# Top-k attention with a phase mixer: work three units ahead, marks in tiles of two batches, one step fewer in the weights' conversion, the sums' constant added by GpSimd

## The chip, the cores and the metric

The kernel runs on one NeuronCore of one Trainium2 chip. The time is the device time of one execution, in microseconds; lower is better. The kernel before takes 1268.95 us, the median of three runs (1268.45 to 1269.72).

## The reference

There are 8 batches, 8 heads, 576 positions and 64 channels per head; the mixer works on 512 channels. Everything is float32 at the reference's level; the four weight matrices reach the kernel as 64-bit floats and are converted on the chip.

```python
scores = scale * np.matmul(q, k.transpose(0, 1, 3, 2))
kth = np.partition(scores, -top_k, axis=-1)[..., -top_k:-top_k + 1]   # top_k = 32
scores = np.where(scores >= kth, scores, -1000000000.0)
scores = scores - np.max(scores, axis=-1, keepdims=True)
attn = np.exp(scores)
attn = attn / (np.sum(attn, axis=-1, keepdims=True) + 1e-09)
x = np.matmul(attn, v)            # then heads side by side: (batch, seq, 512)
theta = x @ w_theta
y = einsum('ts,bsd->btd', w_tok_r, x * np.cos(theta)) + einsum('ts,bsd->btd', w_tok_i, x * np.sin(theta))
u = x + y
return u + np.maximum(u @ w_ch, 0.0)
```

## The kernel before

**Units.** Two heads make a pair, so a batch has 4 pairs. A pair's 576 queries are cut into four blocks of 128 for both heads and one block in which the 64 remaining queries of both heads lie together: five units, of which the last has half the work. There are 160 units. The loop in `pipeline` walks over them; in step `i` different units are at different stages, in the order of the letters in `ORDER`.

**One unit's way.** `scores` multiplies queries and keys on TensorE (PE) in two passes (`kh`, `kl`) into a PSUM tile `ps_score`, of which there are two places, and ScalarE (ACT) copies it to a tile `e` in SBUF (tag `e`, `EBUFS` places, shared with the loaded pairs). `fold` compares quarters of a row on VectorE (DVE) (L295 to L298): the largest of each four go to the list `lst`, the others to `lo1`, which has two places. `pick` takes the best eights of `lo1` into the list (L303). `threshold` ranks the list in four rounds of MAX8 and MATCH_REPLACE8 (L317, L323) and ends with L327; GpSimd (POOL) makes the limits from it (L328). `penalize` has ACT and POOL push the scores below the limit down (L336, L338). `exponent` is on ACT and leaves the sums (L348). `turn` transposes on PE (`pt`, L363) and ACT copies to `at`; `mix_values` multiplies with the values (`px`).

The scores and the fold of unit `i + AHEAD` are issued in step `i`, the pick of unit `i + 1`, the ranking of unit `i`. `FOLDS` is the number of places for `lst`.

**Marks.** A short list could miss a value. POOL copies the smallest entries of each picked eight and the ranks of each unit to `marks`, one slot per head and query block (L304, L330). After the last unit, DVE compares all 288 slots at once and reduces the answer to one flag; a branch redoes everything in a plain way if the flag is set.

**Mixer.** When a batch's attention is done, `mixer` normalizes with the reciprocals of the sums (`rinv`, L446 and L447), computes angles (`pth`, L518), sine and cosine, the token products (`py`, L633; DVE adds them with `settle`, L609) and the output products (`po`, L660; DVE empties them with `give`, L614). It is a generator: `turn` advances it by some matmuls after each transposed head, so a batch's mixer runs beside the next batch's attention. The last batch's mixer has nothing beside it and runs in three passes of halved operands (`halve`, L409 on ACT, L410 on POOL or DVE).

**Weights.** `widen_steps` converts one of 17 weight blocks in each step from the third on. `size` is in PSUM; DVE raises it to `SMALLEST` (L156) and shifts it into the bits of a float32 (L157); POOL puts the parts together (L159, L160).

The order within each engine is not the order of the code: a planner with modelled durations lays out one fixed row of instructions per engine; each engine then works through its row in order.

Of the kernel before, what the change touches and what calls it, by code (L numbers as in the profile page):

```python
# [18 lines left out]
P = 128  # L19
EBUFS = 10  # L20
NQP = 1
WSTART = 2
AHEAD = 2
# [3 lines left out]
FOLDS = 3  # L27
BESTS = 4
M_TOK = 400
# [8 lines left out]
SMALLEST = 1.125 * 2.0  # L38
# [6 lines left out]
def topk_attention_phase_mixer(  # L45
# [30 lines left out]
    NSLOT = B * NPAIR * (2 * NJ + 1)  # L76
# [17 lines left out]
    marks = const.tile([P, NSLOT, NE + 4], F32, name="marks")  # L94
    nc.gpsimd.memset(marks[:, :, :NE], -1.0)
    nc.gpsimd.memset(marks[:, :, NE:], 0.0)
# [21 lines left out]
    def widen_steps():  # L118
# [26 lines left out]
        def convert(i):  # L145
# [7 lines left out]
            for c in range(0, n, m):  # L153
                size = ps_m.tile([P, 512], F32, tag="m", name="size")[:, :m]
                nc.scalar.activation(size, sign[:, c : c + m], AF.Abs, scale=2.0**16)
                nc.vector.tensor_scalar(size, size, SMALLEST, None, op0=ALU.max)  # L156
# [143 lines left out]
    def pick(u):  # L300
        for i, (lo, hi) in enumerate(EXTRA):
            for w in range(u.n):
                nc.vector.max(u.lst[:, w, QS + i * 8 : QS + i * 8 + 8], u.lo1[:, w, lo:hi])  # L303
        nc.gpsimd.tensor_copy(marks[:, u.slot : u.slot + u.n, :NE], u.lst[:, : u.n, QS + 7 :: 8])  # L304
# [4 lines left out]
    def threshold(u):  # L309
# [19 lines left out]
        if not u.full:  # L329
            nc.gpsimd.tensor_copy(marks[:, u.slot : u.slot + n, NE:], top[:, :n, 7 : LB - 1 : 8])  # L330
        yield

# [107 lines left out]
    def mixer(bt, split=False, beside=False):  # L440
# [4 lines left out]
        for rows, js in ((P, slice(0, NJ)), (REM, slice(NJ, NJ + 1))):  # L445
            nc.vector.tensor_scalar(rinv[:rows, js], sums[:rows, js], 1e-9, None, op0=ALU.add)  # L446
            nc.vector.reciprocal(rinv[:rows, js], rinv[:rows, js])  # L447
# [228 lines left out]
    def pipeline():  # L676
# [5 lines left out]
        def unit(i):  # L682
            if not 0 <= i < total:
                return None
            if i not in units:
# [4 lines left out]
                units[i] = Unit(b, batches[b], p, j, pairs[g], g * (2 * NJ + 1) + 2 * j, False)  # L690
# [30 lines left out]
        for i in range(total + 3):  # L721
# [30 lines left out]
            for c in ORDER:  # L752
                steps[c]()
            if i == 0:
# [8 lines left out]
        worst = const.tile([P, 1], F32, name="worst")  # L763
        flag_f = const.tile([1, 1], F32, name="flag_f")
        kept = const.tile([P, 1], F32, name="kept")
        over = wk2.tile([P, NSLOT, NE + 3], BF16, tag="lo1", name="over")
        nc.vector.tensor_tensor(
            over,
            marks[:, :, : NE + 3],
            marks[:, :, NE + 3 :].to_broadcast([P, NSLOT, NE + 3]),  # L770
            op=ALU.is_ge,
        )
        nc.vector.tensor_reduce(kept, over[:, :, NE:], axis=AX.XY, op=ALU.min)
        nc.vector.tensor_reduce(worst, over[:, :, :NE], axis=AX.XY, op=ALU.max)
        nc.vector.tensor_tensor(worst, worst, kept, op=ALU.is_ge)
        pf = ps_m.tile([P, 512], F32, tag="m", name="pf")
# [74 lines left out]
```

## Time and profile before

| | |
|---|---|
| median of three runs | 1268.95 us (1268.45 to 1269.72) |
| profiled execution | 1273.75 us |
| its span, first to last instruction | 1271.9 us |
| busy: PE, DVE, ACT, POOL | 1137.0, 1139.2, 1021.9, 686.0 us |
| mean granted clock of PE | 0.953 of full speed |
| 0 to 260 us | attention of batch 0 and the weights, then the first mixer starts |
| 260 to 1118 us | attention of one batch beside the mixer of the one before |
| from 1177 us | transposes of the last units, then the last mixer alone |

Shares over the whole span mix these stages. What matters in each is which engine has no idle time, and what the others wait for. "Busy" of PE contains the modelled ends of overlapping matmuls. Lines such as L446 are lines of the kernel before.

### The profile page before, as it was taken

How to read it: one execution, taken by the hardware profiler on the slowest of the kernel's cores; microseconds unless marked ns; L12 is line 12 of the kernel's file. 1: busy time of each engine (PE TensorE's matmuls, PEld its weight loads, DVE VectorE, ACT ScalarE, POOL GpSimd, SP SyncE). 2: the span in 40 equal slices, each digit the busy share in tenths (PEclk: the TensorE clock that was granted, in tenths of full speed). 3: DMA queues.
4: the chain of work that ended last, by engine and by line, in shares of the span. 5: the costliest groups of instructions: out<-in, count | busy, mean ns of one | idle time of the engine just before them, and what ended most of it. 6: DMA issues, size and time to landing. Idle time of an engine off the chain costs nothing.

```text
span 1271.9 us, 23007 instructions
## 1 busy us (share of the span) xinstructions
PE 1137.0 (89%) x6293; PEld 849.5 (67%) x6293; DVE 1139.2 (90%) x5049; ACT 1021.9 (80%) x2098; POOL 686.0 (54%) x944
## 2 busy tenths in 40 slices
PE   3666679799999998999989998999999998998998
PEld 3554455578667875687657775677757775676688
DVE  7999999989999899989999799989999899988263
ACT  4999888987799868997789868997879868996361
POOL 2677774763565535664456444664546535756130
PEclk7677789899999999999999999999999999999899
DMA  7255432332323133332322233323313333200001
GB/s 198 73 159 159 118 92 63 93 85 76 113 70 81 53 106 94 93 84 76 113 56 75 66 113 94 93 67 94 112 32 84 82 103 103 74 10 1 38 2 40
DMA packets 71020, 106.14 MB, mean 83 GB/s; under 512 B 13920, under 2 KB 32608, under 8 KB 70880
## 3 DMA queue, kind: packets, MB, share of 16 engines
q1 hardware_dynamic: 70880, 104.57, 30.1%
q8 instruction: 52, 0.85, 0.3%
q14 instruction: 88, 0.72, 0.2%
HBM read 38.40 MB, written 9.44 MB: 38 GB/s over the span
## 4 chain that ended last, share of the span: by engine, by line
PE 44%; DVE 29%; ACT 15%; DMA 4%; POOL 3%; issue 3%; SPq 1%; ACTq 0%; POOLq 0%; DVEq 0%
PE py L633 17%; PE px L393 7%; PE ps_score L259 6%; DVE lst L323 6%; DVE best L317 6%; DVE lst L303 5%; PE pt L363 5%; PE pth L518 5%; ACT e L348 3%; DVE lo L296 3%; PE po L660 2%; ACT e L268 2%; ACT pen L336 2%; POOL e L338 2%; DVE ps_score L295 2%
## 5 line engine op out<-in xcount | busy, mean ns | idle before, releaser
L338 POOL TENSOR_TENSOR e<-e,pen 128x576 f32<-128x576 f32 x288 | 365.5, 1285 | 153.9 <-ACT pen L336 152.9
L317 DVE MAX8 best<-lst 128x8 f32<-128x122 f32 (+3 forms) x1152 | 286.1, 287 | 0.7
L633 PE MATMUL py<-w,z 128*128 128x288 f32 x1008 | 267.4, 408 | 0.2
L348 ACT ACTIVATE e<-e,lim 128x576 f32<-128x576 f32 x288 | 224.7, 782 | 28.9 <-POOL e L338 27.9
L259 PE MATMUL ps_score<-kh,q 128*128 128x288 f32 x512 | 185.2, 377 | 58.5 <-ACT e L268 36.8
L336 ACT ACTIVATE pen<-e,lim 128x576 bf16<-128x576 f32 x288 | 210.2, 776 | 32.3 <-POOL lim L328 31.6
L323 DVE MATCH_REPLACE8 lst<-best,lst 128x122 f32<-128x122 f32 (+2 forms) x864 | 230.9, 273 | 0.0
L363 PE MATMUL pt<-ident,e 128*128 128x128 f32 x1152 | 185.4, 288 | 35.1 <-ACT e L348 31.4
L633 PEld LDWEIGHTS py<-w,z 128*128 128x128 f32 x1008 | 182.5, 191 | 40.9 <-POOL z L550 0.7
L303 DVE MAX8 lst<-lo 128x8 f32<-128x72 f32 (+1 forms) x864 | 209.3, 291 | 0.1
L363 PEld LDWEIGHTS pt<-ident,e 128*128 128x128 f32 x1152 | 143.0, 147 | 76.8 <-ACT e L348 39.4
L268 ACT COPY e<-ps_score 128x576 f32<-128x576 f32 x256 | 161.3, 640 | 30.0 <-PE ps_score L259 22.0
L365 ACT COPY at<-pt 128x512 f32<-128x512 f32 x256 | 148.5, 587 | 35.4 <-PE pt L363 34.5
L393 PE MATMUL px<-at,vt 128*64 128x320 f32 (+1 forms) x1024 | 161.0, 433 | 10.0 <-ACT at L368 7.0
L259 PEld LDWEIGHTS ps_score<-kh,q 128*128 128x128 f32 x512 | 102.1, 199 | 87.2 <-ACT e L268 46.7
L259 PE MATMUL ps_score<-kl,q 128*128 128x288 f32 x512 | 151.7, 311 | 0.0
L660 PE MATMUL po<-xt,w 128*128 128x288 f32 x448 | 127.3, 415 | 6.6 <-DVE ot L614 6.6
L393 PEld LDWEIGHTS px<-at,vt 128*64 128x64 f32 x1024 | 78.8, 144 | 74.2 <-issue 14.3
L296 DVE TENSOR_TENSOR lo<-ps_score,e 128x576 f32<-128x576 f32 (+1 forms) x160 | 109.6, 685 | 0.0
L259 PEld LDWEIGHTS ps_score<-kl,q 128*128 128x128 f32 x512 | 103.4, 202 | 5.9 <-issue 1.4
L295 DVE TENSOR_TENSOR ps_score<-ps_score,e 128x288 f32<-128x288 f32 (+1 forms) x160 | 67.9, 424 | 43.5 <-ACT e L268 38.0
L518 PE MATMUL pth<-w,xt 128*128 128x512 f32 x224 | 103.9, 598 | 0.0
(131 smaller groups left out, 1926.6 us busy)
## 6 DMA issues: line engine op xcount, KB each, us to landing
kh<-hi SPq DMA_DIRECT2D x124, 144.0 KB, 2.6
kl<-raw SPq DMA_DIRECT2D x124, 144.0 KB, 2.6
raw<-in_qT_dram SPq DMA_DIRECT2D x31, 288.0 KB, 3.0
raw<-in_kT_dram SPq DMA_DIRECT2D x31, 288.0 KB, 3.2
q<-hi SPq DMA_DIRECT2D x62, 144.0 KB, 2.6
q<-raw SPq DMA_DIRECT2D x62, 144.0 KB, 2.7
vt<-in_v_dram SPq DMA_DIRECT2D x32, 256.0 KB, 3.2
out_dram<-ot SPq DMA_DIRECT2D x28, 288.0 KB, 2.1
```

Of the source, the lines that this page charges most:

```text
L259: nc.tensor.matmul(out[:, at : at + n], l, r, start=(i == 0), stop=(i == len(mm) - 1), skip_group_check=True)
L268: nc.scalar.copy(u.x[:, :, keys], u.ps[:, :, :HS])
L303: nc.vector.max(u.lst[:, w, QS + i * 8 : QS + i * 8 + 8], u.lo1[:, w, lo:hi])
L317: nc.vector.max(top[:, w, best], part[w])
L323: nc.vector.match_replace(out=rest, in_to_replace=top[:, w, best], in_values=part[w], imm_value=LOWEST)
L336: nc.scalar.activation(pen[:, w], u.x[:, w], AF.Relu, bias=u.lim[:, w, 0:1], scale=-STEEP)
L338: nc.gpsimd.tensor_sub(u.x[:, w], u.x[:, w], pen[:, w])
L348: nc.scalar.activation(u.x[:, w], u.x[:, w], AF.Exp, bias=u.lim[:, w, 1:2], scale=SCALE, accum_out=acc)
L363: fixed(nc.tensor.transpose(pt[:, c], e[:, w, at0 : at0 + P], ident))
L393: nc.tensor.matmul(px[sl, :n], pr["vt"][:, kb, sl], pr["at"][:, a, kb], start=(kb == 0), stop=False, skip_group_check=True)
L518: fill(nc.tensor.matmul(th[j][: l.shape[-1]], l, r, **pos))
L633: fill(nc.tensor.matmul(py[:, :HS], l, r, start=(i == 0), stop=(i == len(mm) - 1)))
```

## The change

There are five parts. `AHEAD` goes from 2 to 3, with one more place for `e` tiles and one more for lists. `marks` is no longer one constant tile of 288 slots, but a tile of 72 slots for two batches, of which two are alive; `judge` compares and reduces one such tile two steps after its last unit, so four times, and a short reduction joins the four answers at the end. The two memsets of `marks` go. In the weights' conversion ACT scales by another power of two, with which DVE's raising (L156) is left out. In the mixer, the constant 1e-9 is added to the sums by POOL in place, with a broadcast tile `least`, and DVE only takes the reciprocal.

```diff
-EBUFS = 10
+EBUFS = 11
...
-AHEAD = 2
+AHEAD = 3
...
-FOLDS = 3
+FOLDS = 4
 BESTS = 4
+MARKED = 2
...
-SMALLEST = 1.125 * 2.0
...
-    NSLOT = B * NPAIR * (2 * NJ + 1)
+    NSLOT = MARKED * NPAIR * (2 * NJ + 1)
...
-    marks = const.tile([P, NSLOT, NE + 4], F32, name="marks")
-    nc.gpsimd.memset(marks[:, :, :NE], -1.0)
-    nc.gpsimd.memset(marks[:, :, NE:], 0.0)
+    worst = const.tile([P, B // MARKED], F32, name="worst")
+    kept = const.tile([P, B // MARKED], F32, name="kept")
+    least = const.tile([P, 1, 1], F32, name="least")
+    nc.vector.memset(least, 1e-9)
...
-                nc.scalar.activation(size, sign[:, c : c + m], AF.Abs, scale=2.0**16)
-                nc.vector.tensor_scalar(size, size, SMALLEST, None, op0=ALU.max)
+                nc.scalar.activation(size, sign[:, c : c + m], AF.Abs, scale=2.0**-112)
                 nc.vector.tensor_scalar(bits[:, c : c + m], size.bitcast(I32), 3, None, op0=ALU.logical_shift_left)
...
-        nc.gpsimd.tensor_copy(marks[:, u.slot : u.slot + u.n, :NE], u.lst[:, : u.n, QS + 7 :: 8])
+        if u.slot == 0:
+            u.batch["marks"] = wk2.tile([P, NSLOT, NE + 4], F32, tag="marks", name="marks")
+        nc.gpsimd.tensor_copy(u.batch["marks"][:, u.slot : u.slot + u.n, :NE], u.lst[:, : u.n, QS + 7 :: 8])
...
+    def judge(marks, i):
+        over = wk2.tile([P, NSLOT, NE + 3], BF16, tag="lo1", name="over")
+        nc.vector.tensor_tensor(
+            over,
+            marks[:, :, : NE + 3],
+            marks[:, :, NE + 3 :].to_broadcast([P, NSLOT, NE + 3]),
+            op=ALU.is_ge,
+        )
+        nc.vector.tensor_reduce(kept[:, i : i + 1], over[:, :, NE:], axis=AX.XY, op=ALU.min)
+        nc.vector.tensor_reduce(worst[:, i : i + 1], over[:, :, :NE], axis=AX.XY, op=ALU.max)
...
         for rows, js in ((P, slice(0, NJ)), (REM, slice(NJ, NJ + 1))):
-            nc.vector.tensor_scalar(rinv[:rows, js], sums[:rows, js], 1e-9, None, op0=ALU.add)
-            nc.vector.reciprocal(rinv[:rows, js], rinv[:rows, js])
+            tiny = least[:rows].to_broadcast([rows, js.stop - js.start, H])
+            nc.gpsimd.tensor_add(sums[:rows, js], sums[:rows, js], tiny)
+            nc.vector.reciprocal(rinv[:rows, js], sums[:rows, js])
...
+            done = unit(i - 2)
+            if done and done.j == NJ and done.p == NPAIR - 1 and done.bq % MARKED == MARKED - 1:
+                judge(done.batch["marks"], done.bq // MARKED)
...
-        over = wk2.tile([P, NSLOT, NE + 3], BF16, tag="lo1", name="over")
...
-        nc.vector.tensor_reduce(kept, over[:, :, NE:], axis=AX.XY, op=ALU.min)
-        nc.vector.tensor_reduce(worst, over[:, :, :NE], axis=AX.XY, op=ALU.max)
         nc.vector.tensor_tensor(worst, worst, kept, op=ALU.is_ge)
+        nc.vector.tensor_reduce(worst[:, :1], worst, axis=AX.X, op=ALU.max)
```

Lines of the changed kernel are shifted: its L319, L325, L329 are L317, L323, L327 of before, L351 is L338, L423 is L410, L455 is L442, L461 is L447, L494 is L480, L623 is L609, L628 is L614; its L460 is the new addition.

**Conversion.** DVE's row where the second weight block is converted, first of the kernel before. `lst` and `best` belong to units that are being ranked, numbers tell the units apart.

```order
L323 MATCH_REPLACE lst_439<-best_440,lst_439 128x102
L156 TENSOR_SCALAR size_463<-size_463 128x512
L323 MATCH_REPLACE lst_439<-best_440,lst_439 128x102
L295 TENSOR_TENSOR lo1_531<-ps_score_523,e_516 128x2x144
L296 TENSOR_TENSOR lo1_531<-ps_score_523,e_516 128x2x288
L327 TENSOR_REDUCE best_291<-best_291 128x2
L317 MAX best_364<-lst_363 128x8
L317 MAX best_440<-lst_439 128x8
L157 TENSOR_SCALAR room_228<-size_463 128x512
```

The same place of the changed kernel:

```order
L325 MATCH_REPLACE lst_315<-best_316,lst_315 128x158
L297 TENSOR_TENSOR lst_461<-ps_score_455,lo1_463 128x2x144
L298 TENSOR_TENSOR lo1_463<-ps_score_455,lo1_463 128x2x144
L157 TENSOR_SCALAR room_251<-size_485 128x512
L303 MAX lst_461<-lo1_463 128x8 x2
L325 MATCH_REPLACE lst_386<-best_387,lst_386 128x102 x2
L329 TENSOR_REDUCE best_223<-best_223 128x2
```

The instruction L156 between ACT's `size` and the shift L157 is gone; the shift stands between the fold and the pick of a unit.

**Middle.** DVE's row in the third batch, kernel before, from the last rounds of one unit (list 6709) to the first of the next (list 6800):

```order
L323 MATCH_REPLACE lst_6709<-best_6710,lst_6709 128x158 x2
L317 MAX best_6710<-lst_6709 128x8 x2
L609 TENSOR_TENSOR xt_4022<-py_6425,xt_4022 128x288
L327 TENSOR_REDUCE best_6710<-best_6710 128x2
L295 TENSOR_TENSOR ps_score_6794<-ps_score_6794,e_6787 128x2x144
L295 TENSOR_TENSOR lo1_6802<-ps_score_6794,e_6787 128x2x144
L296 TENSOR_TENSOR lo1_6802<-ps_score_6794,e_6787 128x2x288
L297 TENSOR_TENSOR lst_6800<-ps_score_6794,lo1_6802 128x2x144
L298 TENSOR_TENSOR lo1_6802<-ps_score_6794,lo1_6802 128x2x144
L303 MAX lst_6800<-lo1_6802 128x8 x2
L317 MAX best_6801<-lst_6800 128x8 x2
L303 MAX lst_6800<-lo1_6802 128x8 x4
```

The changed kernel, from the pick of one unit (list 6546) on:

```order
L303 MAX lst_6546<-lo1_6548 128x8 x2
L319 MAX best_6547<-lst_6546 128x8 x2
L303 MAX lst_6546<-lo1_6548 128x8 x4
L325 MATCH_REPLACE lst_6546<-best_6547,lst_6546 128x102 x2
L295 TENSOR_TENSOR ps_score_6617<-ps_score_6617,e_6610 128x2x144
L319 MAX best_6547<-lst_6546 128x8 x2
L295 TENSOR_TENSOR lo1_6625<-ps_score_6617,e_6610 128x2x144
L296 TENSOR_TENSOR lo1_6625<-ps_score_6617,e_6610 128x2x288
L325 MATCH_REPLACE lst_6546<-best_6547,lst_6546 128x122 x2
L297 TENSOR_TENSOR lst_6623<-ps_score_6617,lo1_6625 128x2x144
L298 TENSOR_TENSOR lo1_6625<-ps_score_6617,lo1_6625 128x2x144
L303 MAX lst_6623<-lo1_6625 128x8 x2
```

Before, a unit's fold, pick and four rounds stand in one piece and the next unit's fold follows. Now the next unit's fold (list 6623) stands between the second and the third round. In PE's row 234 score matmuls stand ahead of the first angle matmul of the first mixer in both kernels, and 276 before and 284 now ahead of its first token matmul.

**End of attention, DVE.** DVE's row from the last reduction of the last unit's ranking on, kernel before:

```order
L327 TENSOR_REDUCE best<-best 128x1
L609 TENSOR_TENSOR xt<-py,xt 128x288
L767 TENSOR_TENSOR over<-marks 128x1728
L446 TENSOR_SCALAR rinv<-sums 128x32
L773 TENSOR_REDUCE kept<-over 128x1
L774 TENSOR_REDUCE worst<-over 128x1
L447 RECIPROCAL rinv<-rinv 128x32
L775 TENSOR_TENSOR worst<-worst,kept 128x1
L609 TENSOR_TENSOR xt<-py,xt 128x288
L446 TENSOR_SCALAR rinv<-sums 64x8
L447 RECIPROCAL rinv<-rinv 64x8
L614 SCALAR_TENSOR_TENSOR ot<-po,xt 128x288 x8
```

The changed kernel, from the same reduction on:

```order
L329 TENSOR_REDUCE best<-best 128x1
L623 TENSOR_TENSOR xt<-py,xt 128x288
L337 TENSOR_TENSOR over<-marks 128x432
L343 TENSOR_REDUCE kept<-over 128x1
L344 TENSOR_REDUCE worst<-over 128x1
L783 TENSOR_TENSOR worst<-worst,kept 128x4
L784 TENSOR_REDUCE worst<-worst 128x1
L623 TENSOR_TENSOR xt<-py,xt 128x288
L461 RECIPROCAL rinv<-sums 128x32
L623 TENSOR_TENSOR xt<-py,xt 128x288
L461 RECIPROCAL rinv<-sums 64x8
L628 SCALAR_TENSOR_TENSOR ot<-po,xt 128x288 x4
```

The additions L446 have left DVE; the comparison has a quarter of the slots; three instructions `xt<-py` stand behind the last ranking instead of two.

**End of attention, POOL.** POOL's row from the last unit's last penalty on, kernel before; L410 is the subtraction that halves weights:

```order
L338 TENSOR_TENSOR e<-e,pen 128x576
L410 TENSOR_TENSOR w<-w,w_hi 128x576
L410 TENSOR_TENSOR w_lo<-w_215,w_hi 128x512
L442 COPY sums<-sums_rem 64x4
L410 TENSOR_TENSOR w<-w,w_hi 128x576
L410 TENSOR_TENSOR w_14287<-w_216,w_hi 128x512
```

The changed kernel, from the penalties of the last two units on:

```order
L351 TENSOR_TENSOR e<-e,pen 128x576 x2
L460 TENSOR_TENSOR sums<-sums,least 128x32
L351 TENSOR_TENSOR e<-e,pen 128x576
L423 TENSOR_TENSOR w<-w,w_hi 128x576
L423 TENSOR_TENSOR w_lo<-w_238,w_hi 128x512
L423 TENSOR_TENSOR w<-w,w_hi 128x576
L455 COPY sums<-sums_rem 64x4
L423 TENSOR_TENSOR w_14277<-w_239,w_hi 128x512
L423 TENSOR_TENSOR w<-w,w_hi 128x576
L460 TENSOR_TENSOR sums<-sums,least 64x8
```

The addition on 64x8 sums stands behind the copy of the sums and two more subtractions of weights.

## Rows read from the trace of the kernel before

**Rows 1.** The page, part 1: busy us, share of the span, instructions.

```profile
PE 1137.0 (89%) x6293; PEld 849.5 (67%) x6293; DVE 1139.2 (90%) x5049; ACT 1021.9 (80%) x2098; POOL 686.0 (54%) x944
```

**Rows 2.** Busy time by stage: columns in the first line.

```profile
core 0: us, PE busy (x) PEld busy (x) DVE busy (x) ACT busy (x) POOL busy (x), PEclk, DMA share, GB/s
27.00:175.00 148.00, 95.05 (x457) 70.00 (x456) 144.33 (x651) 132.59 (x275) 105.56 (x132) 0.73 0.46 129
175.00:260.00 85.00, 72.26 (x376) 50.76 (x376) 82.41 (x391) 75.34 (x154) 53.22 (x80) 0.92 0.28 73
260.00:1118.00 858.00, 817.13 (x4602) 604.48 (x4601) 806.13 (x3690) 719.09 (x1483) 463.03 (x658) 1.00 0.32 85
1118.00:1177.00 59.00, 55.12 (x295) 42.40 (x294) 50.30 (x188) 45.29 (x97) 38.54 (x50) 0.99 0.02 6
1177.00:1272.00 95.00, 86.53 (x530) 72.99 (x528) 37.70 (x66) 35.74 (x69) 16.94 (x13) 0.95 0.07 27
```

**Rows 3.** Who TensorE waited for, 27 to 260 us: total, times, longest.

```profile
PE pt L363 <- ACT e L348: 30.1, 19, 5.8
PE ps_score L259 <- ACT e L268: 19.2, 14, 3.2
```

**Rows 4.** Who TensorE waited for, 260 to 1118 us.

```profile
PE ps_score L259 <- ACT e L268: 14.9, 15, 1.9
```

**Rows 5.** Who VectorE waited for, 260 to 1118 us.

```profile
DVE ps_score L295 <- ACT e L268: 31.5, 29, 2.9
```

**Rows 6.** Groups by line and shape: count, busy, mean ns, idle before.

```profile
L259 PE MATMUL ps_score<-kh,q 128*128 128x288 f32 x512 | 185.2, 377 | 58.5 <-ACT e L268 36.8 <-DVE q L208 8.7 <-DVE lo L298 8.6
...
L156 DVE TENSOR_SCALAR size<-size 128x288 f32<-128x288 f32 x18 | 8.3, 463 | 1.8 <-ACT size L155 1.8
...
L446 DVE TENSOR_SCALAR rinv<-sums 128x32 f32<-128x32 f32 x8 | 6.2, 778 | 0.9 <-ACT e L348 0.6
...
L446 DVE TENSOR_SCALAR rinv<-sums 64x8 f32<-64x8 f32 x8 | 6.2, 770 | 3.6 <-POOL sums L442 3.6
...
L156 DVE TENSOR_SCALAR size<-size 128x512 f32<-128x512 f32 x8 | 5.5, 690 | 1.1 <-ACT size L155 1.1
```

**Rows 7.** Timeline of VectorE in the first stage: start, us, instruction.

```profile
46.53 0.70 DVE L156 TENSOR_SCALAR size<-size 128x512 f32<-128x512 f32 x1
47.13 0.09 DVE L323 MATCH_VALUE_LOAD lst<-best,lst 128x8 f32 x1
```

**Rows 8.** Timeline of VectorE at the end of attention.

```profile
1160.32 1.96 DVE L767 TENSOR_TENSOR over<-marks 128x1728 bf16<-128x1728 f32 x1 [0.37 <-POOL marks L330]
...
1163.51 1.04 DVE L773 TENSOR_REDUCE kept<-over 128x1 f32<-128x864 bf16 x1
...
1170.55 5.16 DVE L446 TENSOR_SCALAR rinv<-sums 64x8 f32<-64x8 f32 x1 [3.61 <-POOL sums L442]
...
1175.95 0.82 DVE L614 SCALAR_TENSOR_TENSOR ot<-po,xt 128x288 f32<-128x288 f32 x2
```

**Rows 9.** Timeline of GpSimd at the end of attention.

```profile
1160.84 5.71 POOL L410 TENSOR_TENSOR w<-w,w_hi 128x576 fp32r<-128x576 f32 x3 [0.40 <-ACT w_hi L409]
1166.50 1.29 POOL L338 TENSOR_TENSOR e<-e,pen 128x576 f32<-128x576 f32 x1
1167.73 1.42 POOL L410 TENSOR_TENSOR w<-w,w_hi 128x576 fp32r<-128x576 f32 x1
1169.10 1.29 POOL L410 TENSOR_TENSOR w_lo<-w,w_hi 128x512 fp32r<-128x512 f32 x1
1170.31 0.20 POOL L442 COPY sums<-sums_rem 64x4 f32<-64x4 f32 x1
1170.46 6.57 POOL L410 TENSOR_TENSOR w<-w,w_hi 128x576 fp32r<-128x576 f32 x5
```

**Rows 10.** Timeline of TensorE at the end of attention.

```profile
1176.46 1.33 PE L660 MATMUL po<-xt,w 128*128 128x288 f32 x2 [3.88 <-DVE ot L614]
```

**Rows 11.** Busy time in the stretch after that wait, columns as above.

```profile
1176.40:1182.50 6.10, 6.04 (x16) 4.40 (x17) 0.83 (x3) 0.59 (x1) 0.63 (x1) 0.50 0.12 48
```

**Rows 12.** One line's instructions: min, median, max ns, first and last start.

```profile
L157 DVE TENSOR_SCALAR room<-size x26: 439/455/685, 15.3 to 173.9; 128x288 int32<-128x288 int32 x18, 128x512 int32<-128x512 int32 x8
```

More of the change, by code (lines that the diff above doesn't have):

```diff
@@ L329, in threshold @@
         if not u.full:
-            nc.gpsimd.tensor_copy(marks[:, u.slot : u.slot + n, NE:], top[:, :n, 7 : LB - 1 : 8])
+            nc.gpsimd.tensor_copy(u.batch["marks"][:, u.slot : u.slot + n, NE:], top[:, :n, 7 : LB - 1 : 8])
         yield
+    def judge(marks, i):
[8 more added lines that the diff above has]
+        nc.vector.tensor_reduce(worst[:, i : i + 1], over[:, :, :NE], axis=AX.XY, op=ALU.max)
     def penalize(u):
@@ L689, in unit @@
                     batches[b] = new_batch(b)
-                units[i] = Unit(b, batches[b], p, j, pairs[g], g * (2 * NJ + 1) + 2 * j, False)
+                    if b % MARKED:
+                        batches[b]["marks"] = batches[b - 1]["marks"]
+                units[i] = Unit(b, batches[b], p, j, pairs[g], (g * (2 * NJ + 1) + 2 * j) % NSLOT, False)
             return units[i]
@@ L762, in pipeline @@
                 split(g + 2)
-        worst = const.tile([P, 1], F32, name="worst")
         flag_f = const.tile([1, 1], F32, name="flag_f")
-        kept = const.tile([P, 1], F32, name="kept")
-        over = wk2.tile([P, NSLOT, NE + 3], BF16, tag="lo1", name="over")
[L767 to L772, printed above, removed]
-        nc.vector.tensor_reduce(kept, over[:, :, NE:], axis=AX.XY, op=ALU.min)
-        nc.vector.tensor_reduce(worst, over[:, :, :NE], axis=AX.XY, op=ALU.max)
         nc.vector.tensor_tensor(worst, worst, kept, op=ALU.is_ge)
+        nc.vector.tensor_reduce(worst[:, :1], worst, axis=AX.X, op=ALU.max)
         pf = ps_m.tile([P, 512], F32, tag="m", name="pf")
-        nc.tensor.transpose(pf[:1, :P], worst, ident)
+        nc.tensor.transpose(pf[:1, :P], worst[:, :1], ident)
         nc.vector.reduce_max(flag_f, pf[:1, :P], axis=AX.X)
```

## The prediction

> **What bounds the kernel now.** I read the page's busy times first, then the busy times by stage, then who waited for whom in each stage, and last the rows of the few microseconds in which TensorE stood still near the end. Over the whole span TensorE (PE) and VectorE (DVE) are level at 89% and 90% [rows 1], which says nothing about which of them sets the time; the stages do [rows 2].
>
> From 27 to 175 us only attention runs, together with the conversion of the weights. DVE is busy for 144.3 of 148 us, ScalarE (ACT) for 132.6, PE for 95.1. DVE sets the pace there. PE's waits are for scores' copies and exponentials, that is for what DVE releases late [rows 3]. From 175 to 260 us DVE is still at 82.4 of 85. From 260 to 1118 us the mixer of one batch runs beside the attention of the next: PE is busy for 817.1 of 858 us at a granted clock of 1.00, so 40.9 us of gaps are all that can be won there without less matmul work. The largest named gap is PE waiting for a PSUM place of scores that ACT empties, 14.9 us [rows 4]. DVE has 51.9 us of idle time there, 31.5 of it spent waiting for scores [rows 5]: it is the hungry engine, not the limit. After 1177 us PE alone matters: 86.5 of 95 us.
>
> So a microsecond taken from DVE is worth up to a microsecond before 260 us, and close to nothing after it, unless PE waits for that very instruction. A shorter first stage is kept to the end, because the PE work that follows is the same and starts sooner.
>
> **Raising of sizes removed.** Twenty-six instructions go, 18 of 463 ns and 8 of 690 ns, together 13.8 us busy [rows 6]. They overlap their successor: one that started at 46.53 and lasted 0.70 was followed at 47.13 [rows 7], so 0.10 us of each is not DVE's time, and 26 x 0.10 = 2.6 comes off: 11.2 us. One of them runs before 27 us, where DVE had gaps: some 10.6 us lie in the DVE-bound stage. If DVE stays the bound, the stage shrinks by all of it, to 137.4 us; ACT's 132.6 us would then be 97% of it. Two engines that feed each other do not both run so full: in the stage from 260 us PE and DVE share the load at 95% and 94%. At 94 to 95% for both, 132.6 us of ACT and 133.7 of DVE (144.3 less 10.6) need about 140.5 us. That is a gain of **7.5 us**. Ends: 2 (ACT and the weights' transfers, which go through the same two places of `room`, take over at once) and 11.
>
> **Three units ahead.** When the first token matmul stands in PE's row, 284 score matmuls stand before it instead of 276. The eight are one unit's, at 377 ns mean with overlap [rows 6], at most 3 us and back to back nearer 1, moved from the full stage into one where PE idles a third of the time. I take **1 us**. In the middle, the order shows the fold of the next unit between the rounds of the present one, where before each unit was folded, picked and ranked in one piece. This takes DVE's hunger away, but DVE is not the limit there. PE gains only where its 40.9 us of gaps close. I take **2 us**, with 15 (all waits of the kind in [rows 4]) as the lower end of the time and a loss, priced with the rivals, as the upper. The new tile place and the fourth list place cost no instruction. `lo1` keeps two places, so the fold of unit i+3 must follow the pick of unit i+1 on DVE; both are on the same engine in that order, so no wait is added.
>
> **Marks judged four times.** One comparison of 1728 elements took 1.96 us and each of two reductions 1.04 [rows 8]. A quarter of the slots makes about 0.5 + 0.3 + 0.3 = 1.1 us; three such sets now lie inside the body, 3.3 us of DVE time under 51.9 us of idle: nothing. If that cover were gone, 3.3 us. Each set waits for a marks copy by GpSimd (POOL) that is two units old, so it should not block. The two memsets at the start go from POOL, which nobody waits for.
>
> The comparison reads two SBUF operands. While it ran, three POOL subtractions that began at 1160.84 took 5.71 us instead of 3 x 1.42 [rows 8, 9]. So either engine can lose about 1.4 us to each set: with 3 sets 4.2 us at most, under the same cover. The Trainium skill (SBUF — State Buffer, "Who interferes with whom") has a rule that speaks against this part: a DVE instruction with two SBUF inputs contends with a GpSimd instruction that reads SBUF. The trace agrees; by the rule alone three more encounters in the body would be charged, by the row they are hidden.
>
> **The sums' constant.** Sixteen additions leave DVE, 6.2 + 6.2 = 12.4 us [rows 6]. Half of that is two instructions of the last batch, above all one of 5.16 us on 64x8 elements: it starts at 1170.55, POOL runs five subtractions back to back from 1170.46, and the addition ends only at 1175.71 [rows 8, 9]. Behind it stands the reciprocal, and behind that the instruction that empties a PSUM place of the output projection, for which PE waits 3.88 us [rows 10]. PE then runs from 1176.4 to 1182.5 at a granted clock of 0.50, its level of 1.2 GHz, after having stood idle [rows 11]; at full clock those 6.04 us of work would take 3. Price of the whole stall: 3.9 + 3.0 = 6.9 us.
>
> What takes its place is an addition on POOL in POOL's order. After the last unit's penalty is subtracted, three subtractions, the copy of sums, two more subtractions and the addition follow: 1.42 + 1.29 + 1.42 + 0.20 + 1.42 + 1.29 + 0.2 = 7.2 us, using the durations of [rows 9]. Before, the same distance was from 1167.79 to 1175.71, 7.9 us. So by distance alone only 0.7 us is won; the wait turns from a blocked instruction into a queue. But in the order of the changed kernel three `settle` instructions stand on DVE behind the last ranking instead of two, each with nine matmuls ahead of it. Attention thus ends earlier against the mixer, and the queue has some microseconds more to drain unseen. I take half of the stall, **3.5 us**, ends 0 and 6.9. The other fourteen additions, about 6 us over the body, are DVE time in PE's stage: nothing, at most 6. On POOL sixteen additions of about 0.2 us [rows 9] add 3 us to an engine with room.
>
> **Sum.** 7.5 + 1 + 2 + 3.5 = 14 us. The profiled execution took 1273.75 us, 1.85 more than its span and 4.8 more than the median of the runs shown. 1273.75 becomes about 1259.7; from the median, 1268.95 - 14 = **1255 us**.
>
> **Rivals.** *The body's gaps close too.* DVE works ahead, folds come early, and PSUM places of scores free up: the 14.9 us of [rows 4] go, less the 2 already counted. Time: 1255 - 13 = 1242. Against it: those places wait for ACT's copies, and ACT's queue is not touched. Chance 0.15.
>
> *ACT holds the first stage.* The conversion is a chain through ACT, DVE and POOL, and with DVE faster the others are at their own pace. Only the tail and the moved matmuls remain: 4.5 us, or 6.5 with the first stage's lower end: 1262 to 1265. Chance 0.16.
>
> *It does not reach the end at all.* PE holds equally many score matmuls (234) ahead of the mixer's first angle in both orders, so three ahead is not three ahead there, and POOL's queue keeps the tail as it was. What is won early would be lost in new gaps: 1267 to 1271. Chance 0.08.
>
> *Slower: late turns.* With the next fold set between the rounds of the present unit, a unit's last ranking comes later after its first, and penalty, exponential and PE's transposes follow it. PE's transposes stand at a fixed place; if the exponential is late, everything behind waits. In the first 260 us that happened 19 times for 30.1 us, 1.6 us each [rows 3]. Some 120 units pass from 260 to 1118 us. Nine new waits eat the gain of 14 us, eleven make it slower, one in each of 24 pairs costs 38 us: 1255 + 38 = 1293. For it: the folds do stand between the rounds. Against it: a unit now has one more unit of lead to spend. Chance 0.11.
>
> **How the numbers follow.** The forecast, 1249 to 1261, has 0.50. Differences under 0.2% (2.5 us) cannot be told from none in these measurements. Faster: 0.50 + 0.15 + 0.16 = 0.81; same 0.08; slower 0.11. The range leaves out the slower case, and beyond 1243 about half of the best one: 1243 to 1268.
>
> **What would show it.** The conversion's last shift should start near 167 instead of 173.9 us [rows 12], with DVE still above 93% from 27 us on; if instead DVE falls under 92% and the end stays, the second rival holds. PE's busy share from 260 us on should stay at 95%. At the end, no DVE instruction of 64x8 elements should last over 0.5 us, and PE's wait for the emptied place should be under 2 us; if the reciprocal waits over 3 us for POOL, the tail term is wrong. PE waits for exponentials after 260 us, now almost absent, would show the slower case. The prediction fails if PE's gaps in the middle stage move by more than 10 us either way.

## The result and the profile after

The changed kernel takes 1258.38 us, the median of seven runs (1253.26 to 1261.08), against 1269.72 of the kernel before, also of seven: a ratio of 0.9905, 95% interval 0.9883 to 0.9927. It is faster, 3.4 us above the forecast of 1255. The profiled execution took 1256.43 us. Its page, part 1, and its busy time by stage, in the stages of [rows 1, 2]:

```profile
PE 1138.1 (91%) x6293; PEld 847.9 (68%) x6293; DVE 1117.9 (89%) x5018; ACT 1016.3 (81%) x2098; POOL 686.5 (55%) x958
```

```profile
27.00:175.00 148.00, 102.29 (x482) 72.24 (x481) 143.79 (x680) 136.96 (x290) 111.86 (x145) 0.75 0.50 135
175.00:260.00 85.00, 76.16 (x405) 53.95 (x406) 81.82 (x378) 76.92 (x157) 52.74 (x74) 0.96 0.28 73
260.00:1118.00 858.00, 818.73 (x4589) 605.73 (x4586) 805.00 (x3698) 713.82 (x1476) 464.61 (x674) 0.99 0.33 85
1118.00:1177.00 59.00, 59.00 (x322) 44.52 (x322) 33.43 (x137) 44.87 (x97) 38.16 (x46) 1.00 0.05 16
1177.00:1255.00 78.00, 70.05 (x463) 61.73 (x461) 35.62 (x62) 29.99 (x58) 12.74 (x9) 0.98 0.07 25
```

VectorE (DVE) is as full as before in the first stage, but the stage is shorter. The instructions of the shift line, the last of which started at 173.9 us in [rows 12]:

```profile
L157 DVE TENSOR_SCALAR room<-size x26: 433/452/691, 13.3 to 158.4; 128x288 int32<-128x288 int32 x18, 128x512 int32<-128x512 int32 x8
```

Fixed windows mix different work once a kernel runs earlier. So I cut each trace at the same two matmuls: the first of the second half of batch 0's token products, and the first transposes of the seventh mixer. The matmuls are the same 6293 in every kernel here, so over the whole span what a kernel's TensorE (PE) loses is idle time (width less busy) or half clock (more busy time). The parts do not hold quite equal work: the attention's matmuls stand a little differently around the cuts (the counts behind the busy times). Kernel before, then the changed one; columns as in [rows 2]:

```profile
0.00:275.10 275.10, 193.16 (x953) 140.82 (x953) 258.30 (x1167) 235.38 (x480) 178.02 (x237) 0.81 0.43 118
275.10:1062.90 787.80, 751.72 (x4239) 559.64 (x4239) 739.59 (x3388) 655.18 (x1354) 420.96 (x604) 1.00 0.31 85
1062.90:1271.90 209.00, 192.12 (x1105) 149.07 (x1103) 141.30 (x497) 131.30 (x266) 87.02 (x104) 0.97 0.11 33
```

```profile
0.00:265.10 265.10, 195.42 (x956) 139.43 (x957) 249.00 (x1147) 232.66 (x479) 175.52 (x236) 0.85 0.44 118
265.10:1056.10 791.00, 756.64 (x4241) 562.71 (x4239) 741.47 (x3406) 657.36 (x1363) 428.14 (x622) 0.99 0.33 86
1056.10:1254.70 198.60, 186.04 (x1099) 145.73 (x1099) 127.48 (x467) 126.31 (x258) 82.88 (x101) 0.99 0.12 34
```

The first part gained 10.0 us (PE idle 81.9 before, 69.7 after), the middle lost 3.2, the end gained 10.4: 17.2 in the two spans. Of these some 6 are luck of the two profiled executions: before's stood 4.0 above the median of its seven runs, after's 2.0 below its own. In the middle PE's idle time did not grow (36.1 and 34.4 us); its busy time did, by 4.9 us, and by the clock's records it stood at 0.50 for 17.1 us there instead of 3.4.

PE's waits from 27 to 260 us, where the first and the third line answer to [rows 3] (30.1 and 19.2 us), and from 260 to 1118, to be read beside [rows 4]. `px_s` and `px_t` are the PSUM places of the mixer's transposes, `z` is the tile that DVE normalizes (L494):

```profile
PE pt L376 <- ACT e L361: 14.8, 8, 4.0
PE pq L386 <- ACT at L378: 9.8, 7, 2.4
PE ps_score L259 <- ACT e L268: 8.5, 12, 1.7
...
PE px_s L595 <- DVE z L494: 5.7, 4, 3.1
PE px_s L595 <- ACT at L378: 3.6, 5, 2.0
PE px_t L509 <- DVE z L494: 3.4, 3, 1.7
PE ps_score L259 <- ACT e L268: 3.2, 5, 1.7
```

The wait for scores' places fell from 14.9 to 3.2 us in the middle, and another took its place: the mixer's first transposes wait until DVE has normalized. The end of attention, first the reciprocal on 64x8 sums on DVE, then GpSimd (POOL) around the addition, then PE:

```profile
1160.85 0.20 DVE L461 RECIPROCAL rinv<-sums 64x8 f32<-64x8 f32 x1 [3.32 <-POOL sums L460]
1162.55 0.46 DVE L628 SCALAR_TENSOR_TENSOR ot<-po,xt 128x288 f32<-128x288 f32 x1 [1.51 <-PE po L674]
```

```profile
1157.87 0.18 POOL L455 COPY sums<-sums_rem 64x4 f32<-64x4 f32 x1
1158.02 2.63 POOL L423 TENSOR_TENSOR w<-w,w_hi 128x512 fp32r<-128x512 f32 x2
1160.62 0.19 POOL L460 TENSOR_TENSOR sums<-sums,least 64x8 f32<-64x8 f32 x1
1160.78 8.19 POOL L423 TENSOR_TENSOR w<-w,w_hi 128x512 fp32r<-128x512 f32 x6
```

```profile
1160.41 2.59 PE L674 MATMUL po<-xt,w 128*128 128x288 f32 x10
1162.84 0.60 PE L376 MATMUL pt<-ident,e 128*128 128x128 f32 x4
```

DVE waits 3.32 us for POOL, the reciprocal takes 0.20 (against 5.16 of the addition in [rows 8]), and PE has no gap there: its 3.88 us of [rows 10] and the half clock of [rows 11] are gone.

### The profile page after: what moved, and what is told of

Read it like the earlier page. It is cut to its first block, busy times and chain, and to the rows that moved or that the text cites. A ratio compares the mean times of both kernels' runs of the same rounds, so it can differ in the third digit from the quotient of the medians.

```text
span 1254.7 us, 22863 instructions
## 1 busy us (share of the span) xinstructions
PE 1138.1 (91%) x6293; PEld 847.9 (68%) x6293; DVE 1117.9 (89%) x5018; ACT 1016.3 (81%) x2098; POOL 686.5 (55%) x958
## 4 chain that ended last, share of the span: by engine, by line
PE 41%; DVE 28%; ACT 18%; DMA 4%; POOL 4%; issue 3%; SPq 1%; ACTq 0%; DVEq 0%; POOLq 0%
PE py L647 13%; PE pth L532 7%; DVE best L319 6%; DVE lst L325 6%; PE px L406 5%; PE ps_score L259 5%; DVE lst L303 5%; ACT e L361 5%; PE pt L376 4%; ACT pen L349 3%; DVE lo L296 3%; ACT e L268 3%; PE po L674 2%; POOL e L351 2%; DVE ps_score L295 2%
## 5 line engine op out<-in xcount | busy, mean ns | idle before, releaser
L351 POOL TENSOR_TENSOR e<-e,pen 128x576 f32<-128x576 f32 x288 | 365.8, 1285 | 129.8 <-ACT pen L349 127.2
L319 DVE MAX8 best<-lst 128x8 f32<-128x102 f32 (+3 forms) x1152 | 287.2, 291 | 9.7 <-POOL lim L330 9.2
L325 DVE MATCH_REPLACE8 lst<-best,lst 128x102 f32<-128x102 f32 (+2 forms) x864 | 232.4, 277 | 0.1
L376 PE MATMUL pt<-ident,e 128*128 128x128 f32 x1152 | 181.1, 283 | 27.0 <-ACT e L361 14.8
L378 ACT COPY at<-pt 128x512 f32<-128x512 f32 x256 | 148.2, 589 | 36.1 <-PE pt L376 35.5
L406 PE MATMUL px<-at,vt 128*64 128x320 f32 (+1 forms) x1024 | 164.0, 437 | 5.6 <-ACT at L381 3.1
L674 PE MATMUL po<-xt,w 128*128 128x288 f32 x448 | 124.0, 408 | 1.0 <-DVE ot L628 0.8
L532 PE MATMUL pth<-w,xt 128*128 128x512 f32 x224 | 109.7, 623 | 0.0
```

What stands on the lines that cost most here:

```text
L319: nc.vector.max(top[:, w, best], part[w])
L325: nc.vector.match_replace(out=rest, in_to_replace=top[:, w, best], in_values=part[w], imm_value=LOWEST)
L351: nc.gpsimd.tensor_sub(u.x[:, w], u.x[:, w], pen[:, w])
L376: fixed(nc.tensor.transpose(pt[:, c], e[:, w, at0 : at0 + P], ident))
L406: nc.tensor.matmul(px[sl, :n], pr["vt"][:, kb, sl], pr["at"][:, a, kb], start=(kb == 0), stop=False, skip_group_check=True)
L532: fill(nc.tensor.matmul(th[j][: l.shape[-1]], l, r, **pos))
```

## The experiments

The chip's runs come in three groups of four. In the first, theory A is that of the prediction (a first stage paced by DVE, an end held by the blocked addition), and theory B that the rows which three units ahead bring make both gains. Letters for the parts: R, raising removed; S, sums' constant on POOL; A, three units ahead; M, marks in tiles. "First", "middle" and "end" are the widths of the three windows cut as above, in us; "idle" is PE's idle time in the first two; "PE" is its busy time in the whole span. They are of one execution each, up to 4.3 us from its kernel's median. A ratio is that to the kernel before in the same group (its median is 1270.4 in the first, 1271.0 in the second, 1270.2 in the third); the changed kernel's is that of the result.

| kernel | parts | median us | ratio, 95% interval | first | middle | end | idle first, middle | PE |
|---|---|---|---|---|---|---|---|---|
| before | none | 1270.4 | 1 | 275.1 | 787.8 | 209.0 | 81.9, 36.1 | 1137.0 |
| changed | R S A M | 1258.4 | 0.9905 (0.9883 to 0.9927) | 265.1 | 791.0 | 198.6 | 69.7, 34.4 | 1138.1 |
| e1 | R | 1258.7 | 0.9908 (0.9894 to 0.9922) | 260.7 | 794.9 | 205.0 | 68.2, 38.1 | 1138.3 |
| e2 | S | 1278.9 | 1.0078 (1.0065 to 1.0091) | 278.2 | 797.1 | 200.4 | 79.6, 39.8 | 1143.1 |
| e3 | A M | 1279.1 | 1.0085 (1.0067 to 1.0102) | 279.1 | 794.0 | 201.8 | 83.9, 35.8 | 1140.4 |
| e4 | R S M | 1274.2 | 1.0026 (1.0011 to 1.0042) | 259.3 | 808.0 | 200.8 | 69.9, 48.7 | 1135.8 |
| f1 | S A M | 1273.6 | 1.0019 (1.0002 to 1.0037) | 283.8 | 786.6 | 201.5 | 83.8, 32.4 | 1142.6 |
| f2 | R A M | 1263.0 | 0.9936 (0.9913 to 0.9959) | 261.2 | 800.6 | 198.1 | 70.0, 38.0 | 1139.5 |
| f3 | M | 1286.8 | 1.0118 (1.0091 to 1.0144) | 275.2 | 799.4 | 213.7 | 80.0, 39.3 | 1148.3 |
| f4 | none, pace 8.501 | 1280.4 | 1.0082 (1.0056 to 1.0108) | 274.9 | 792.1 | 211.4 | 77.3, 38.2 | 1145.1 |
| g4 | none, pace 8.45 | 1279.2 | 1.0068 (1.0048 to 1.0088) | 277.3 | 798.2 | 204.6 | 81.0, 39.4 | 1144.0 |
| g1 | R S | 1259.7 | 0.9916 (0.9900 to 0.9931) | 258.9 | 800.4 | 200.4 | 68.8, 40.6 | 1137.3 |
| g2 | R S A M, pace 8.501 | 1270.4 | 0.9997 (0.9985 to 1.0010) | 262.8 | 804.9 | 199.0 | 68.4, 40.9 | 1143.0 |
| g3 | R S A M, products first | 1262.3 | 0.9936 (0.9916 to 0.9956) | 263.7 | 795.2 | 200.5 | 70.3, 33.2 | 1143.7 |

A has no kernel without M. What it does beside M is seen in two pairs that differ in A alone (f3 and e3, e4 and changed).

**e1, the raising alone** (kernel before).

```diff
-nc.scalar.activation(size, sign[:, c : c + m], AF.Abs, scale=2.0**16)
-nc.vector.tensor_scalar(size, size, SMALLEST, None, op0=ALU.max)
+nc.scalar.activation(size, sign[:, c : c + m], AF.Abs, scale=2.0**-112)
```

> The kernel before with the raising of sizes left out and nothing else. Theory A (the first stage is bound by VectorE, and the tail by the blocked addition): the first token product of batch 0 is reached 7 to 11 us sooner, the stall at the end of attention stays, total 7 to 11 us less, ratio 0.991 to 0.9945. Theory B (the new row order from three units ahead brings the gains of both ends): at most 2 us less, ratio 0.998 to 1.0.

Measured: the whole gain, from the first part (275.1 to 260.7), a little more than theory A's 0.991 to 0.9945. Its last shift:

```profile
L156 DVE TENSOR_SCALAR room<-size x26: 427/455/682, 13.2 to 157.8; 128x288 int32<-128x288 int32 x18, 128x512 int32<-128x512 int32 x8
```

So the first part's gain is R's; B falls there. The end still has the blocked addition, and PE waits 2.06 us for the place behind it.

**e2, the addition on POOL alone** (kernel before).

```diff
-nc.vector.tensor_scalar(rinv[:rows, js], sums[:rows, js], 1e-9, None, op0=ALU.add)
-nc.vector.reciprocal(rinv[:rows, js], rinv[:rows, js])
+nc.gpsimd.tensor_add(sums[:rows, js], sums[:rows, js], tiny)
+nc.vector.reciprocal(rinv[:rows, js], sums[:rows, js])
```

> The kernel before with the sums' constant added by GpSimd and nothing else. Theory A: the addition of 5.16 us on VectorE is gone, TensorE's wait of 3.88 us and the stretch at half clock behind it go or shrink, 4 to 9 us less, ratio 0.993 to 0.997; nothing changes before 1100 us by more than 2 us. Theory B (attention must also end earlier against the mixer, which comes from three ahead): the reciprocal waits for GpSimd's queue as long as it was blocked before, at most 1.5 us less, ratio 0.9985 to 1.001.

Measured: the end is 8.6 us shorter, and PE waits for no emptied place there; yet the kernel is 0.8% slower, which neither theory allowed: the middle lost 9.3, the first part 3.1. PE is busy 6.1 us longer with the same matmuls.

**e3, three ahead and marks** (the changed kernel with the two edits above undone).

> The changed kernel with the raising of sizes and VectorE's addition put back: three ahead, and marks in tiles. Theory A: the first stage is as before, in the middle TensorE waits more for the normalized tile (some 10 us against 5) and partly runs at half clock behind it, 0 to 5 us more, ratio 1.0 to 1.004; the stall at the end may shrink by the earlier end of attention. Theory B: 8 to 14 us less, ratio 0.989 to 0.994.

Measured: nothing gained in the first part, 7.2 us gained at the end with the addition still on DVE, 6.2 lost in the middle, and slower in all, by more than theory A's 0.4%. The addition now waits for one subtraction only (1.22 us) and PE doesn't wait behind it. So A, with M, also ends the stall; some 3 of the 7.2 us are 16 matmuls fewer behind the cut (1089 against 1105, at 0.17 us each).

**e4, two ahead** (the changed kernel).

```diff
-EBUFS = 11
+EBUFS = 10
-AHEAD = 3
+AHEAD = 2
-FOLDS = 4
+FOLDS = 3
```

> The changed kernel with two units ahead, ten places and three lists: raising gone, constant on GpSimd, marks in tiles. Theory A: both gains stay and the loss in the middle goes, 14 to 20 us less than before, ratio 0.984 to 0.989. Theory B: the gains go with the lead, 1 to 5 us less than before, ratio 0.996 to 0.999.

Measured: slower than before, outside both theories. Against the changed kernel the first part is 5.8 us shorter, the end 2.2 and the middle 17 us longer. I could not yet tell a merit of A from chance: all four kernels had lost in the middle, whatever was edited. In the second and third group theory A is that each part has its price, and theory B that the planner's new rows decide.

**f1, the raising back** in the changed kernel, **f2, the addition back on DVE** in it, and **f3, marks alone** in the kernel before; the edits are those above and the `marks` lines of the change.

> The changed kernel with the raising of sizes put back on VectorE; three ahead, four judgements and the sums' constant on GpSimd stay. Theory A (three causes that add up: the first stage is paced by VectorE and the raising costs TensorE 12 us of idle time there; three units ahead keeps TensorE's idle time in the middle at 34 to 36 us where two ahead leaves 38 to 49; the addition on GpSimd takes 2 to 3 us of idle time from the end): TensorE idle up to the second half of the first batch's token products 80 to 84 us instead of 69.7, middle and end as in the changed kernel, time 1258.4 + 12 = 1268 to 1272. Theory B (the planner's new rows decide, by chance, and the parts have no effect of their own): the time lies anywhere between 1258 and 1280, and the middle's idle time differs from the changed kernel's by more than 5 us.

> The changed kernel with the addition of the sums' constant put back on VectorE; the rest stays. Theory A: idle time of TensorE in the first stage near 70 us, middle 34 to 36 us, end 2 to 4 us more than in the changed kernel, time 1260 to 1264, that is about 1258.4 plus the blocked addition's 3 us; VectorE's addition on 64x8 sums in the last batch lasts over 1 us. Theory B: no such addition is blocked at the end, or the time differs from 1258.4 by more than 6 us through the middle.

> The kernel before with the marks in tiles of two batches, judged four times, and nothing else of the change. Theory A: three judgements in the body lie in VectorE's idle time, so TensorE's idle time stays within 4 us of before in each of the three parts and the time is 1270 to 1275. Theory B: as with the other single parts that gained nothing, the new rows cost 5 to 10 us: 1275 to 1281, most of it in the middle.

**f4, a nudge** to the kernel before, with no instruction added or removed.

```diff
-RATE = 8.5
+RATE = 8.501
```

> The kernel before with the mixer's pace at 8.501 instead of 8.5 matmuls for each transposed head: no instruction is added or removed, only the places of some matmuls of the mixer in the rows shift, and the planner lays out new rows. Theory A: 1270.4, within 3 us. Theory B (chance of the rows): off by 5 to 10 us either way, which is the yardstick for what a single part's difference means.

Measured: f1 lost 15 us against the changed kernel, with PE idle for 83.8 us in the first part instead of 69.7; that is theory A, 1.6 us beyond its time. f2's time is within theory A (4.7 us lost), but none of it is lost at the end, where A had put it. f3 took 1286.8 us, above both theories, and 0.4% more than the nudge; three hidden judgements, forecast at 1.1 us each, don't explain 16 us. And f4 lost 0.82% by itself:

```profile
0.00:274.90 274.90, 197.64 (x952) 141.83 (x953) 257.97 (x1165) 234.79 (x479) 177.75 (x237) 0.83 0.43 118
274.90:1067.00 792.10, 753.91 (x4241) 559.50 (x4240) 743.73 (x3394) 655.11 (x1357) 421.06 (x604) 1.00 0.31 85
1067.00:1278.40 211.40, 193.59 (x1105) 149.67 (x1103) 143.29 (x493) 130.47 (x264) 85.79 (x104) 0.96 0.11 32
```

Idle time is 133.3 us (134.9 before), but PE is busy 8.1 us longer. Theory B holds as to the size of chance: a single difference of 0.8% in the whole time says nothing about a part. What can be told apart is a stage's own number that no other edit moves.

**g1, raising and sums, two ahead and one tile of marks** (the edits of e1 and e2 together).

> The kernel before with the raising removed and the sums' constant added by GpSimd; two units ahead and one tile of marks as before. Theory A (each part has its own price, and the rows of the kernel before are a lucky draw worth some 9 us that any new planning gives away): the raising alone gave 1258.7 with an addition that VectorE was blocked in; with the addition on GpSimd TensorE's time from the seventh mixer's first transposes to the end falls from 205 to about 200 us: 1252 to 1256, faster than the whole change. Rival (three units ahead earns its place in the middle): TensorE's idle time in the middle is 38 to 49 us instead of 34, time 1260 to 1274, slower than the whole change. Theory B (each planning is a draw of its own): anywhere from 1250 to 1275.

**g2, the same nudge** to the changed kernel, and **g4, another nudge** to the kernel before (8.45).

> The changed kernel with the mixer's pace at 8.501 instead of 8.5 matmuls for each transposed head; nothing else. Theory A (only the kernel before has uncommonly good rows): 1255 to 1262, within 4 us of the changed kernel's 1258.4. Theory B (the changed kernel's rows are a lucky draw too, as the pace's nudge to the kernel before cost 9 us): 1264 to 1272. TensorE's idle time up to the first batch's second token products stays at 68 to 71 us under both, since the raising is gone.

> The kernel before with the mixer's pace at 8.45 instead of 8.5 matmuls for each transposed head: a second new planning of the same work. Theory A: 1276 to 1284 again, since the rows of the kernel before are better than new ones, with TensorE's busy time over 1142 us instead of 1137 (more stretches at half the granted clock). Theory B (each planning is a draw around the same mean): on either side of 1270.7, by up to 9 us.

**g3, the normalizing products first.** The changed kernel with the planner's rank of L494 raised:

```diff
-                nc.vector.tensor_tensor(
+                with tc.high_priority(offset=600):
+                    nc.vector.tensor_tensor(
```

> The changed kernel in which the planner ranks the mixer's normalizing products on VectorE 600 places earlier, so that they stand ahead of the ranking of units; no instruction is added or removed. If VectorE's backlog makes TensorE wait for the emptied place of the mixer's first transposes (25.8 us of gaps at px_s and px_t in the changed kernel, 9.7 in the kernel before), those gaps fall under 14 us, the middle's idle time from 34 to under 28 us, and the time to 1250 to 1255. If the wait only moves to another instruction of the ranking or of the scores, the middle stays at 33 to 38 us and the time at 1256 to 1264.

Measured: g1 is as fast as the whole change, within both intervals, so A and M together are not shown to bring anything; its time misses theory A's 1252 to 1256 and lies just under the rival's 1260 to 1274, and its idle time in the middle, 40.6 us, is the rival's. g2 loses 0.92%, as theory B had it, g4 0.68%, which fits both its theories: both kernels' rows are better than nudged ones, and the changed kernel's middle shows it (g2, middle row):

```profile
262.80:1067.70 804.90, 763.97 (x4255) 569.05 (x4254) 748.11 (x3426) 656.00 (x1367) 427.87 (x623) 0.98 0.32 85
```

Nudged against nudged, the change is worth 1280.4 or 1279.2 against 1270.4, some 9 to 10 us, close to the 11 to 12 between the two kernels themselves. g3 did not shorten the middle. Some of its waits there, 260 to 1060 us (its lines are one further):

```profile
PE px_s L596 <- DVE z L495: 4.0, 3, 1.8
...
PE px_s L596 <- ACT at L378: 3.0, 4, 2.0
...
PE px_s L596 <- ACT xt L511: 2.4, 2, 1.7
```

The wait moved in part from DVE to ACT, as the second expectation had it; PE's idle time in the middle is 33.2 us (34.4 in the changed kernel), and its busy time over the span 5.6 us longer. PE's own gaps at `px_s` and `px_t` from 260 to 1060 us are 12.4 us, against 14.5 in the changed kernel and 6.7 before; the 25.8 and 9.7 of the expectation are larger than these. No version beat the changed kernel; e1 and g1 equal it.

## Why the prediction was right, and where its sum was not

**What bounds the kernel.** A microsecond off DVE is worth a microsecond before 260 us: right. PE's idle time in the first part is 68 to 70 us in the seven kernels without the raising and 77 to 84 in the seven with it, with nothing between, nudged kernels included; the mean width of that part is 261.7 us against 277.7.

**Raising removed, forecast 7.5 us: mis-sized, 12 to 16.** The four pairs of kernels that differ in R alone (before and e1, e2 and g1, e3 and f2, f1 and changed) give 0.92, 1.62, 1.49 and 1.14%, in the mean 1.3% or 16 us. PE's idle time in the first part is 12 of them (the means are 81.1 and 69.3); where the rest comes from is open. The mean busy time of PE there is 4.3 us shorter too, but in part because 8 to 14 fewer matmuls stand before the cut in those pairs. DVE's busy time over the span fell by 7.5 to 13.8 us in the pairs, 10.4 in the mean: the 10.6 of the prediction were right, and the gain was no share of them but all, and more. The term that was mis-sized rests on "two engines that feed each other do not both run so full": I took 94 to 95% from PE and DVE, in another stage. Up to the last shift DVE was still at 127.29 of 131.5 us in the changed kernel, 97%, with ACT at 92%:

```profile
27.00:158.50 131.50, 88.94 (x413) 62.72 (x414) 127.29 (x602) 120.57 (x252) 100.61 (x128) 0.73 0.51 140
```

The last shift came 15.5 us sooner, not 7; that is more than the removed work, because the row has less else before it too (DVE was busy for 143.33 us from 27 us to the last shift in the kernel before, 16.0 more). The second rival (ACT holds the stage) falls with it.

**Three ahead, 1 us at the front: not seen.** In the four pairs that differ in A and M (before and e3, e2 and f1, e1 and f2, g1 and changed) the first part is 0.5 to 6.2 us longer; the 8 to 15 more matmuls before the cut (966 against 953 in e3) are a part of it. **2 us in the middle: not told apart from chance;** the whole times of those pairs differ by +0.85, -0.59, +0.28 and -0.11%. That these cancel may hide two effects. The two pairs that differ in A alone (f3 and e3, e4 and changed) give -0.33 and -1.21%, with the middle 5.4 and 17.0 us shorter; the two that differ in M alone (before and f3, g1 and e4) give +1.18 and +1.10%, with the middle 11.6 and 7.6 us longer. A gain by A and a loss by M is thus a rival that the runs leave open; each is of the size of a nudge or little more.

The wait that I named fell from 14.9 to 3.2 us, and this goes with A: from 260 to 1060 us it is 2.3 to 5.5 us in the six kernels with A and 6.6 to 13.3 in the eight without. Other losses took its room. In the changed kernel the normalizing product waits in DVE's row, behind the ranking of one unit and amid the fold of the next; that the interleaving is the cause is not shown, as e2, with two ahead, has 6.5 us of the same wait. Near 335 us, DVE, then PE, then the stretch around them:

```profile
334.96 0.25 DVE L325 MATCH_REPLACE8 lst<-best,lst 128x102 f32<-128x102 f32 x1
335.13 0.68 DVE L494 TENSOR_TENSOR z<-px_s,rinv 128x512 f32<-128x512 f32 x1
335.73 0.45 DVE L295 TENSOR_TENSOR lo<-ps_score,e 128x288 f32<-128x288 f32 x1
336.09 0.75 DVE L296 TENSOR_TENSOR lo<-ps_score,e 128x576 f32<-128x576 f32 x1
336.75 0.68 DVE L494 TENSOR_TENSOR z<-px_s,rinv 128x512 f32<-128x512 f32 x1
```

```profile
333.23 1.19 PE L595 MATMUL px_s<-ident,xt 128*128 128x128 f32 x8
335.87 0.66 PE L509 MATMUL px_t<-ident,z 128*128 128x128 f32 x4 [1.45 <-DVE z L494]
337.49 0.84 PE L595 MATMUL px_s<-ident,xt 128*128 128x128 f32 x4 [0.97 <-DVE z L494]
339.28 0.47 PE L509 MATMUL px_t<-ident,z 128*128 128x128 f32 x1 [0.94 <-ACT xt L510]
```

```profile
333.00:336.00 3.00, 1.55 (x14) 1.19 (x13) 3.00 (x16) 2.19 (x6) 1.63 (x4) 1.00 0.62 141
336.00:339.00 3.00, 1.37 (x8) 0.73 (x8) 3.00 (x10) 1.80 (x5) 1.31 (x2) 0.80 0.88 194
339.00:342.00 3.00, 2.72 (x5) 1.39 (x6) 3.00 (x16) 2.43 (x5) 1.18 (x2) 0.50 0.00 0
342.00:345.00 3.00, 3.00 (x7) 1.13 (x6) 3.00 (x17) 0.87 (x2) 1.67 (x3) 0.56 0.01 3
```

With three gaps of about a microsecond, 3.4 us in all, the clock falls to 0.50, the level of 1.2 GHz, for nearly seven microseconds (0.80, 0.50 and 0.56 in the last three rows); that costs some 3 us more, so a gap is paid for nearly twice. The prediction had no term for it in the middle. It is one of two ways in which new rows lose: f4 lost by more busy time at the same idle time, e4 by idle time (48.7 us in the middle against 34.4). My sign of failure, gaps in the middle that move by more than 10 us, did not appear, 40.9 to 39.3 us; it could not see this, because half clock counts as busy.

**Marks, forecast nothing.** M alone stands 0.36% above the nudge f4, whose interval overlaps with its own, and 0.50% above g4, whose does not quite. With the pair g1 and e4 (+1.10%) a loss is not excluded, but M's own instructions don't account for it. The four comparisons of the changed kernel:

```profile
L337 DVE TENSOR_TENSOR over<-marks x4: 600/605/1653, 311.1 to 1147.6; 128x432 bf16<-128x432 f32 x4
```

With its two reductions (0.36 and 0.37 us) a set takes 1.3 us. The long comparison is the one that started at 598.98 us, 0.10 us after a POOL subtraction of 1.29 us; beside it the comparison took 1.05 us more, within the 1.4 that I had estimated for a set. In f3, which lost 16 us, all four took 0.60 us.

**Sums' constant, forecast 3.5 us: the place was right, the size and the ground were not.** With A or S or both (nine kernels) the end takes 198.1 to 201.8 us, with neither (five) 204.6 to 213.7; the means are 200.1 and 208.7, so the end gains 8.6, beyond my upper bound of 6.9 (with S but without A, where the matmuls behind the cut are equally many, it is 200.5). PE's wait for the emptied place, 3.88 us before, is 2.06, 4.37 and 5.20 us in e1, f3 and f4 and absent in all nine. It is absent in g4 too, where the addition lasted 5.19 us and the end 204.6: a blocked addition costs only where PE's row stands close behind it, and the end's width has other causes besides. By my own sign, a reciprocal that waits over 3 us for POOL, the tail term was wrong. "The wait turns from a blocked instruction into a queue" happened, 3.32 us of it; that this would hold PE did not, since ten output matmuls follow there without a gap, and the instruction that empties the place (L628) itself waits 1.51 us for PE. Nor was the earlier end of attention needed, on which I let half of the stall go: e2 has the same end (200.4) with two ahead. But the end's 8.6 us do not reach the whole time: the pairs that differ in S alone give +0.78, +0.08, -0.66 and -0.31%, about nothing in the mean, with some 0.3% either way as their scatter leaves it. With two ahead S gains 8.6 and 4.6 us at the end and the middle loses 9.3 and 5.5; with three ahead, where the stall is gone already, the end gains nothing (0.3 and -0.5) and the middle 7.4 and 9.6. Why the middle moves so is not shown; the nudges move it as much.

**Rivals and sum.** Late turns did not come: no wait for an exponential by PE's transposes is among those after 260 us. "The body's gaps close too" was half so: they closed and others opened. The sum of 14 us met 11 to 12, in part by luck: R alone brings as much (e1), where I had given it 7.5, and the other parts together, forecast at 6.5, add nothing to it. In the pair's own spans the front's 8.5 came to 10.0, the end's 3.5 to 10.4, and the middle's gain of 2 to a loss of 3.2; that is 17.2, less the 6 by which the two profiled executions lie apart from their medians.

## What to carry to other kernels

Where a planner lays out rows, first nudge something that adds no work: here that alone moved the time by 0.7 to 0.9%, as much as most of the differences between the kernels above. Judge a part by a number of its own stage (idle time up to the same matmul, the width of the end) in several plannings, and count half clock, which a busy share hides. Where one engine is at 97% and its partner at 90%, as in this first stage, take the full time of what is removed from it, not a share.

## What the runs showed of the hardware

A DVE addition on 64x8 sums lasted 0.14 us at best and, beside POOL's subtractions, up to 7.77. In e1 DVE and then POOL, and the same in f2:

```profile
1159.55 7.77 DVE L445 TENSOR_SCALAR rinv<-sums 64x8 f32<-64x8 f32 x1 [0.90 <-POOL sums L441]
```

```profile
1159.48 9.29 POOL L409 TENSOR_TENSOR w<-w,w_hi 128x512 fp32r<-128x512 f32 x7
```

```profile
1158.24 1.23 DVE L457 TENSOR_SCALAR rinv<-sums 64x8 f32<-64x8 f32 x1 [0.48 <-POOL sums L453]
```

```profile
1158.17 13.79 POOL L421 TENSOR_TENSOR w<-w,w_hi 128x512 fp32r<-128x512 f32 x10
```

In the seven kernels with the addition on DVE, the one on the last batch's 64x8 sums ended 0.02 to 0.03 us after the end of one of POOL's subtractions: the first (e3, f2), the fourth (before, g4) or the sixth (e1, f3, f4). The Trainium skill (SBUF — State Buffer, "Who interferes with whom") says that such a DVE instruction can need the ports shared with GpSimd and that whoever is first holds them for its whole instruction. The traces agree that it waits for the end of an instruction; that up to six pass first, and why the number differs, stays open. The reciprocal on those sums took 0.19 to 0.20 us beside such subtractions (changed kernel, e2, g1).
